# Two output pieces of one head group moved to another sum, with a new order of the work and other streamed weights

## The chip, the cores and the metric

The kernel runs on one core of a Trainium2 chip. TensorE (PE in the profile, with its weight loads as PEld) multiplies into PSUM, VectorE (DVE) and ScalarE (ACT) copy, turn and normalise, GpSimd (POOL) copies small pieces and issues some transfers, and SyncE's queue (SP) issues the large transfers. The metric is the device time of one execution in microseconds; lower is better. The kernel before took 1881.22 us as the median of three runs (1872.94 to 1895.54).

## What is computed

The output has two halves side by side. Half A is a sliding-window attention over 2048 rows; the change leaves it alone. Half B walks over 64 segments of 32 rows. Each segment sees 8 rows of memory ahead of its own 32, and the memory of the next segment is the first 8 rows of this one's output, so the segments run strictly one after the other. Cut to what matters:

```python
mem = mem0                                   # 8 x 640
for s in range(64):
    h = concat([mem, x[32 * s:32 * s + 32]])  # 40 x 640
    q, k, v = h @ Wq, h @ Wk, h @ Wv          # 32 heads of 192
    p = softmax(mask(q @ k.T * scale))        # per head, 40 x 40
    o = (p @ v) @ Wo                          # 6144 x 640, summed over heads
    mem = o[:8]
    out.append(o[8:])
```

## The kernel before

All four weights of half B together are larger than the on-chip memory. They are cut in pieces: for each of four head groups five pieces of Wq, Wk and Wv (128 rows by 1536 columns, 384 KB), and 24 pieces of Wo (320 KB; pieces 0 to 5 belong to head group 0, 6 to 11 to group 1, and so on). Most pieces stay on the chip. The table `STREAMED` (L285) names those that don't: 8 pieces of Wk, 10 of Wv and 5 of Wo, 23 in all, are copied from main memory anew in every segment. `fetch` (L472) issues such a copy on SP's queue into a ring of seven buffers, tile `t`. A copy can therefore start when the piece seven places earlier in the stream has been used for the last time.

One segment works on memory and rows of a segment as 32 new rows (`main`) and as a bundle of 8-row ends that were known early (`ahead`); the bundle is projected for four segments at once, so in each segment one k group and one v group is "renewed" and projected twice (`RENEW`, L288). The order of the work is written out by hand as a list of tokens, `FIRST` for segment 0 and `ORDER` (L298) for the other 63. A token is a step of one head group, and PE, DVE, ACT and SP each run their own instructions in the order of the tokens:

- `q.g`, `k.g`, `v.g`: projections, five pieces each (L561), into one of three PSUM accumulators (`acc`).
- `e.q0` and so on: the copies of accumulators into `QT` or `KT` (L600; the bundle's goes to `sb`, L567). There is one `QT` and one `KT`, so group g + 1 can be copied in only when the scores of group g have been computed. `EVACUATE` (L305) gives the engine of each copy, S for ACT and V for DVE; the first letter is the bundle's copy, which is made in renewed groups alone, and the second the main one.
- `T.q0` and so on: the turning of `QT` or `KT` on DVE (L571), and the late columns by POOL (L607).
- `S.g`: scores on PE (L625). `sb.g`, `mx.g`, `sub.g`, `send.g`: the softmax, on DVE (L631, L638, L642, L647, L648, L657) but for the exponential on ACT (L643). `send.g` writes the tile `P`.
- `tp.g`: P turned by PE (L664). `PT.g`: its spreading, for groups 0 and 1 on ACT (L672) and for groups 2 and 3 on DVE (L675), as `SPREAD` says. `ve.g`: the values copied to `Vst` by ACT (L614).
- `mix.g`: P times V on PE (L688) into two PSUM banks. `ot.g`: these two banks copied as the two halves of `OT` (L696); `HEADS` (L306) names the engine of each half. POOL then collects the late rows of `OT` (L697, L698).
- `out.g.h`: pieces of Wo for group g = 0, 1, 2; h = 0 takes four pieces, h = 1 two (L713). They are summed over the groups in PSUM tile `Y`. A piece has four matmuls of 320 columns. `OT` has twelve slots; pieces 4 and 5 of a group read slots 6 to 11 alone, that is the second half, and the first three pieces of a group read slots 0 to 5 alone.
- `last`: the six pieces of group 3, as 48 matmuls of 160 columns into another layout, `Z` (L739), in a bank of its own.
- `part` (ACT, L720) and `join` (DVE, L725) fold `Y` into the layout of `Z`; the fold lies in `QT`, and its turned form in `KT`. `close` (DVE, L530, L747, L748) turns `Z`, adds the fold, writes the memory rows of the next segment into `HX` and the output rows into `XS`, which POOL sends out (L750). `ql` projects the next q bundle, and the next segment's `q.0` needs what `close` wrote. `tx` (DVE, L530, L541) turns the next segment's rows.

Scores, turned P, mixes and `Z` take their PSUM banks from one ring of four (`bank`), in the order in which they are asked for. A bank is free when its previous content has been read: a score bank when `send` has read it, a mix bank when `ot` has.

Of the kernel before, what the change touches and what calls it, by code (L numbers as in the profile page):

```python
# [23 lines left out]
def part_a(ctx, tc, A_x, A_wqkv, A_wo, out, ident, emit_loads):  # L24
# [241 lines left out]
    with tc.manual_schedule(engines={mybir.EngineType.PE, mybir.EngineType.DVE, mybir.EngineType.Activation}):  # L266
# [4 lines left out]
        for b in range(-1, n_blk):  # L271
# [10 lines left out]

STREAMED = {"q": ((), (), (), ()), "k": ((1, 3), (1, 2), (0, 2), (1, 3)), "v": ((0, 1, 4), (2, 4), (0, 2, 4), (0, 2)),  # L285
            "o": (8, 12, 17, 19, 23)}
PARTS = {}
SLOT = 1536  # L288
RENEW = {0: ("k0", "v2"), 1: ("k1", "v3"), 2: ("k2", "v0"), 3: ("k3", "v1")}
# [6 lines left out]
    ql eql last close Tql  # L296
"""
ORDER = """  # L298
    q.0 e.q0 T.q0 k.0 k.1 e.k0 T.k0 q.1 S.0 sb.0 e.k1 e.q1 mx.0 sub.0 v.0 T.q1 ve.0 T.k1 q.2 S.1 send.0
    e.q2 T.q2 sb.1 mx.1 k.2 tp.0 v.1 e.k2 q.3 PT.0 sub.1 mix.0 T.k2 send.1 tp.1 S.2 ve.1 ot.0 sb.2 e.q3  # L300
    PT.1 mx.2 sub.2 k.3 T.q3 send.2 out.0.0 e.k3 v.2 out.0.1 mix.1 T.k3 S.3 ot.1 tp.2 sb.3 mx.3 v.3 PT.2
    ve.2 mix.2 sub.3 out.1.0 send.3 out.1.1 ot.2 tp.3 ve.3 out.2.0 out.2.1 part tx PT.3 mix.3 ot.3 last
    join ql close eql Tql
"""
EVACUATE = {"k0": "SV", "k1": "SS", "k2": "VS", "k3": "SS", "q0": "VV", "q1": "SS", "q2": "SS", "q3": "VV"}  # L305
HEADS = ("VS", "SV", "VS", "SV")  # L306
SPREAD = "SSVV"
LEAD_IN = 114
HEAD = 10
# [9 lines left out]
def part_b(ctx, tc, B_x, B_mem0, B_Wq, B_Wk, B_Wv, B_Wo, out, ident, n_seg, pre, nbuf, mid):  # L319
    nc = tc.nc  # L320
# [8 lines left out]
    def streamed(u):  # L329
        return u[1] in STREAMED["o"] if u[0] == "o" else u[2] in STREAMED[u[0]][u[1]]  # L330

# [15 lines left out]
    def quarter_cols(u):  # L347
        return 320 if u[0] == "o" else 384
# [11 lines left out]
    def quarter(w, u, i):  # L360

        n = quarter_cols(u)
        if isinstance(w, tuple):
            now = PARTS[u]
            v = w[0][:, n * i:n * i + n] if i < now else w[1][:, n * (i - now):n * (i - now) + n]
            return v.rearrange("p (b c) -> p b c", b=2) if u[0] == "o" else v
        if u[0] == "o":
            return w[:, 640 * (i // 2):640 * (i // 2) + 640].rearrange("p (b g c) -> p g b c", b=2, g=2)[:, i % 2]
        return w[:, n * i:n * i + n]
# [102 lines left out]
    def fetch(u):  # L472
        t = wstream.tile([128, SLOT], BF16, tag="ws")
        nc.sync.dma_start(t[:, 0:stream_cols(u)], copied[u])
        return t[:, 0:stream_cols(u)]
# [3 lines left out]
    def load_pending(u):  # L479
        pending.remove(u)  # L480
        wait.remove(u)
        load_resident([u])

    def get_unit(u):
        if u in wait:
            load_pending(u)
        if not streamed(u):
            return res[u]
        if u in fetched:
            w = fetched.pop(u)  # L490
        else:
            w = fetch(u)
            if pending:
                load_pending(pending[0])
        return (w, res[u]) if u in PARTS else w
# [15 lines left out]
    OT = cpool.tile([128, 12, L], BF16, name="OT")  # L511
# [31 lines left out]
    def bank():  # L543
        return ps_x.tile([128, 512], FP32, tag="x", name="px")
# [50 lines left out]
    def project_qk(s, m, g):  # L595
        return project32([ahead, main] if renewed(s, m, g) else [main], m, g)
# [13 lines left out]
    def values(s, g):  # L610
        return project32([ahead, main] if renewed(s, "v", g) else [main], "v", g)
# [88 lines left out]
    def slot(c):  # L700

        a, k = c // 3, c % 3
        return 6 * (a // 2) + 2 * k + a % 2

    def project_out(Y, g, pairs=range(6)):
        for a in pairs:
            i = 6 * g + a
            w = get_unit(("o", i, 0))
            for r in range(2):
                c = 2 * a + r  # L710
                for gv in range(2):
                    t = 32 * (2 * r + gv)
                    nc.tensor.matmul(Y[t:t + 32].rearrange("p (b c) -> p b c", b=2),  # L713
                                     lhsT=OT[:, slot(c), 0:32], rhs=quarter(w, ("o", i, 0), 2 * r + gv),
                                     start=(i == 0), stop=(i == 17), tile_position=(0, t))

    def join_begin(Y):
        part = QT[:, 0:320].bitcast(FP32)
# [11 lines left out]
        turn32(partT, part)  # L730
        return partT

    def project_last(Y):
        for a in range(6):
            w = get_unit(("o", 18 + a, 0))
            for r in range(2):
                c = 2 * a + r
                for j in range(4):
                    nc.tensor.matmul(Y[32 * j:32 * j + 32], lhsT=OT[:, slot(c), 0:32],  # L739
                                     rhs=quarter(w, ("o", 18 + a, 0), 2 * r + j % 2)[:, j // 2],  # L740
                                     start=(c == 0), stop=(c == 11), tile_position=(0, 32 * j))

    def close(s, Y, part, partT):
        Ysb, T = XS[:], Vst[:, 0:320].bitcast(FP32).rearrange("p (k n) -> p k n", n=SEG)
# [8 lines left out]
    def segment(s):  # L753
        last = s + 1 == n_seg
        engine = {"S": S_, "V": V_}
        got = {}

        def project(m, g):
            if m == "v":
                got["v", g] = values(s, g)  # L760
            else:
                got[m, g] = project_qk(s, m, g)
                if last and (m, g) == ("k", 3):
                    load_late((2, 3))

        def step(name, *at):
            g = int(at[0][-1]) if at else None
            if name in "qkv":
                project(name, g)
            elif name == "e":  # L770
                m = at[0][0]
                got["sb", m, g] = evacuate(m, got.pop((m, g)), [engine[c] for c in EVACUATE[at[0]]])
            elif name == "T":
                m = at[0][0]
                keep = fill_late(s, m, g, got.pop(("sb", m, g)))
                turn_in_place(columns_of(m, 0, 32))
                if m + at[0][1] == "k0" and s and keep:
                    got["keep"] = keep
                elif keep:
                    keep()  # L780
                if at[0] == "k1" and "keep" in got:
                    got.pop("keep")()
            elif name == "S":
                got["S", g] = scores(g)
            elif name == "sb":
                got["t", g] = soft_begin(got.pop(("S", g)))
            elif name == "mx":
                got["mx", g] = soft_max(got["t", g])
            elif name == "sub":
                soft_exp(got["t", g], got.pop(("mx", g)))  # L790
            elif name == "send":
                soft_end(s, g, got.pop(("t", g)))
            elif name == "tp":
                got["p", g] = turn_p(g)
            elif name == "PT":
                got["PT", g] = spread_p(g, got.pop(("p", g)))
            elif name == "ve":
                keep_values(g, got.pop(("v", g)))
                if g == 2:
                    load_x(s + 1)  # L800
                elif last and g == 1:
                    load_late((0, 1))
            elif name == "mix":
                got["mix", g] = mix(g, got.pop(("PT", g)))
            elif name == "ot":
                keep_mix(s, g, got.pop(("mix", g)), [engine[c] for c in HEADS[g]])
            elif name == "out":
                g, half = int(at[0]), int(at[1])
                if "Y" not in got:
                    got["Y"] = ps_y.tile([128, 320], FP32, tag="y", name="Y")  # L810
                project_out(got["Y"], g, range(4 * half, 4 + 2 * half))
            elif name == "part":
                got["part"] = join_begin(got["Y"])
            elif name == "join":
                join_end(got["Y"], got["part"])
                got["partT"] = None if last else turn_part(got["part"])
            elif name == "tx":
                turn_x(s + 1)
            elif name == "ql":
                got["ql"] = None if last else project32([ahead], "q", (s + 1) % 4)  # L820
            elif name == "eql":
                got["sbl"] = None if last else to_sb(got["ql"][0], S_)
            elif name == "last":
                got["Z"] = bank()[:, 0:160]
                project_last(got["Z"])
            elif name == "close":
                close(s, got["Z"], got["part"], got["partT"])
            elif name == "Tql":
                if not last:
                    gl = (s + 1) % 4  # L830
                    turn_late(got["sbl"], "q", gl, s, s + 1)()

        for token in (ORDER if s else FIRST).split():
            step(*token.split("."))
# [3 lines left out]
    def load_late(quads):  # L838
        for b in quads:
            nc.sync.dma_start(res[DEAD[b]], late_o[b].rearrange("p g i c -> p (g i c)"))  # L840
# [143 lines left out]
```

## Time and profile before

| what | value |
|---|---|
| three runs | 1872.94, 1881.22, 1895.54 us |
| the profiled execution, its own time | 1883.37 us |
| its span, first to last instruction | 1881.6 us |
| half A, until half B has its buffers | about 163 us |
| segments 1 to 63, from `last` to `last` | 1608.4 us, 25.53 us each |
| after the last segment (late rows) | 66.4 us |
| PE busy over the span | 1646.5 us, 88% |
| DVE, ACT, POOL busy | 1289.3, 682.5, 680.5 us |
| moved by the transfers | 627.64 MB, 334 GB/s over the span |

How to read it: the busy share of PE counts matmuls that overlap one another and run out in the pipeline, so that 88% doesn't mean that PE can do no more. The segments are one chain, so what matters in them is where PE waits and for whom, and beside it how far the stream of copies is from what the transfer engines can do.

### The profile page before, as it was taken

How to read it: one execution, taken by the hardware profiler on the slowest of the kernel's cores; microseconds unless marked ns; L12 is line 12 of the kernel's file. 1: busy time of each engine (PE TensorE's matmuls, PEld its weight loads, DVE VectorE, ACT ScalarE, POOL GpSimd, SP SyncE). 2: the span in 40 equal slices, each digit the busy share in tenths (PEclk: the TensorE clock that was granted, in tenths of full speed). 3: DMA queues.
4: the chain of work that ended last, by engine and by line, in shares of the span. 5: the costliest groups of instructions: out<-in, count | busy, mean ns of one | idle time of the engine just before them, and what ended most of it. 6: DMA issues, size and time to landing. Idle time of an engine off the chain costs nothing.

```text
span 1881.6 us, 91589 instructions
## 1 busy us (share of the span) xinstructions
PE 1646.5 (88%) x39286; PEld 1043.9 (55%) x39286; DVE 1289.3 (69%) x3671; ACT 682.5 (36%) x1821; POOL 680.5 (36%) x1876
## 2 busy tenths in 40 slices
PE   8998898888888888888888888888889888888887
PEld 5565555555555555555555555555555555555567
DVE  4886677777777777676777777776777777677730
ACT  3454333333333333333333333333333333333310
POOL 3001333344434343433434443433443333444321
PEclk9999999999999999999999999998999999999999
DMA  9926999999999999999999999998999999999991
GB/s 327 317 73 231 388 357 348 360 356 355 348 354 355 355 353 352 340 363 315 361 352 349 363 356 357 372 337 309 369 372 351 360 352 356 333 365 351 348 355 30
DMA packets 276851, 627.64 MB, mean 334 GB/s; under 512 B 60084, under 2 KB 75890, under 8 KB 276444
## 3 DMA queue, kind: packets, MB, share of 16 engines
q1 hardware_dynamic: 257596, 608.42, 90.4%
q0 software_dynamic: 18784, 13.32, 2.3%
q8 instruction: 308, 5.05, 1.1%
q14 instruction: 99, 0.81, 0.1%
q10 hardware_dynamic: 64, 0.04, 0.0%
HBM read 607.47 MB, written 22.91 MB: 335 GB/s over the span
## 4 chain that ended last, share of the span: by engine, by line
PE 54%; DVE 14%; DMA 14%; issue 7%; POOL 6%; ACT 4%; SPq 0%; ACTq 0%; POOLq 0%; DVEq 0%
PE acc L561 27%; DMA t<-wcopy_v 7%; PE Y L713 6%; PE px L625 5%; PE px L688 4%; PE pq L95 3%; DMA late_o<-OL 3%; PE px L739 3%; POOL out_dram L750 2%; DMA t<-wcopy_k 2%; PE px L664 2%; PE px L856 1%; DVE mx L638 1%; DVE px L631 1%; DVE prod L151 1%
## 5 line engine op out<-in xcount | busy, mean ns | idle before, releaser
L561 PEld LDWEIGHTS <-HX 128*32 128x32 bf16 x19380 | 502.3, 97 | 360.2 <-issue 127.0
L561 PE MATMUL acc<-t,HX 128*32 128x384 bf16 x5812 | 435.7, 331 | 32.1 <-DMA t<-wcopy_v 12.6
L561 PE MATMUL acc<-wres_q,HX 128*32 128x384 bf16 x6460 | 326.4, 332 | 22.8 <-issue 11.4
L561 PE MATMUL acc<-wres_k,HX 128*32 128x384 bf16 x3876 | 274.6, 330 | 15.7 <-issue 13.8
L697 POOL COPY OL<-OT 128x96 bf16<-128x96 bf16 x256 | 158.9, 621 | 257.2 <-ACT OT L696 147.8
L561 PE MATMUL acc<-wres_v,HX 128*32 128x384 bf16 x3232 | 215.8, 330 | 2.6 <-issue 2.2
L607 POOL COPY QT<-Lb 128x96 bf16<-128x96 bf16 x252 | 66.7, 265 | 407.0 <-PE px L625 407.0
L696 DVE CAST OT<-px 128x240 bf16<-128x240 f32 x256 | 103.3, 404 | 143.8 <-PE px L688 136.1
L713 PE MATMUL Y<-wres_o,OT 128*32 128x320 bf16 x3840 | 192.7, 302 | 8.6 <-issue 8.3
L625 PE MATMUL px<-KT,QT 64*64 64x40 bf16 (+1 forms) x4096 | 139.3, 189 | 49.6 <-DVE KT L571 23.9
L571 DVE STREAM_TRANSPOSE QT<-QT 128x384 bf16<-128x384 bf16 x256 | 146.6, 573 | 42.2 <-ACT QT L600 40.1
L600 ACT CAST KT<-acc 128x384 bf16<-128x384 f32 x192 | 92.3, 481 | 225.2 <-PE px L625 173.9
L625 PEld LDWEIGHTS <-QT 64*64 64x64 bf16 (+1 forms) x4096 | 108.3, 109 | 111.2 <-issue 46.9
L631 DVE SCALAR_TENSOR_TENSOR px<-px,mask 128x160 f32<-128x160 f32 x256 | 82.7, 323 | 124.0 <-PE px L625 123.7
L698 POOL DMA_DIRECT2D late_o<-OL x256 | 139.4, 545 | 77.9 <-POOL OL L697 60.2
L614 ACT CAST Vst<-acc 128x384 bf16<-128x384 f32 x256 | 123.6, 483 | 110.6 <-PE px L688 87.3
L696 ACT CAST OT<-px 128x240 bf16<-128x240 f32 x256 | 92.4, 361 | 190.0 <-PE px L688 110.7
L567 ACT CAST sb<-acc 128x384 bf16<-128x384 f32 x115 | 55.0, 478 | 262.2 <-PE acc L561 180.5
L713 PEld LDWEIGHTS <-OT 128*32 128x32 bf16 x4608 | 115.1, 97 | 60.7 <-issue 14.4
L571 DVE STREAM_TRANSPOSE KT<-KT 128x384 bf16<-128x384 bf16 x256 | 142.2, 556 | 2.8 <-ACT KT L600 1.2
L750 POOL DMA_DIRECT2D out_dram<-XS x256 | 129.2, 511 | 9.7 <-issue 4.0
L688 PE MATMUL px<-PT,Vst 64*128 64x80 bf16 (+1 forms) x2048 | 123.2, 212 | 9.2 <-issue 6.1
(103 smaller groups left out, 2507.2 us busy)
## 6 DMA issues: line engine op xcount, KB each, us to landing
t<-wcopy_v SPq DMA_DIRECT2D x640, 384.0 KB, 5.9
t<-wcopy_k SPq DMA_DIRECT2D x512, 384.0 KB, 5.5
t<-wcopy_o SPq DMA_DIRECT2D x330, 320.0 KB, 5.3
wres_q<-in_B_Wq_dram SPq DMA_DIRECT2D x20, 384.0 KB, 7.8
late_o<-OL POOLq DMA_DIRECT2D x256, 24.0 KB, 5.1
wres_q<-late_o SPq DMA_DIRECT2D x16, 384.0 KB, 7.3
wres_o<-in_B_Wo_dram SPq DMA_DIRECT2D x19, 320.0 KB, 7.1
wres_k<-in_B_Wk_dram SPq DMA_DIRECT2D x12, 384.0 KB, 7.9
```

The source lines that it names most:

```text
L561: nc.tensor.matmul(ps[n][32 * j:32 * j + 32].rearrange("p (f n) -> p f n", n=32), lhsT=X[:, dc, :], rhs=columns(w, (m, g, dc), j), start=( ...
L571: nc.vector.transpose(t, t)
L600: copies[1](columns_of(m, 0, 32), ps[-1][:].rearrange("p (f n) -> p f n", n=32))
L614: S_(Vst[:], ps[-1][:])
L625: nc.tensor.matmul(Sps[64 * h:64 * h + 64, a, :], lhsT=QT[k0:k1, L * f:L * f + 64], rhs=KT[k0:k1, f, :], start=(outer == 0 and a == 0), st ...
L631: nc.vector.scalar_tensor_tensor(out=Sps, in0=Sps, scalar=scale, in1=mask[:].unsqueeze(1).to_broadcast([128, 4, L]), op0=ALU.mult, op1=ALU ...
L688: nc.tensor.matmul(ps[r][lo:hi, 2 * L * k:2 * L * k + 2 * L], lhsT=V[64 * r:64 * r + 64, col:col + hi - lo], rhs=PT[64 * r:64 * r + 64, 2 ...
L696: copy(OT[:, 6 * r:6 * r + 6].rearrange("p c n -> p (c n)"), ps[r][:, 0:6 * L])
L697: nc.gpsimd.tensor_copy(OL[:, g % 2].rearrange("p n c -> p c n"), OT[:, :, 32:L])
L698: nc.gpsimd.dma_start(late_o[s // 4][:, g, s % 4], OL[:, g % 2].rearrange("p n c -> p (n c)"))
L713: nc.tensor.matmul(Y[t:t + 32].rearrange("p (b c) -> p b c", b=2), lhsT=OT[:, slot(c), 0:32], rhs=quarter(w, ("o", i, 0), 2 * r + gv), sta ...
L750: nc.gpsimd.dma_start(out2[SEG * s:SEG * s + SEG - M, Dm + 160 * j:Dm + 160 * j + 160], Ysb[32 * j + M:32 * j + SEG])
```

## The change

Pieces 16 and 17 of Wo (the last two of group 2, token `out.2.1`) are no longer summed into `Y`. They are written in the layout of `last`, 16 matmuls of 160 columns in place of 8 of 320, into `Z`'s bank, which is now asked for at that token; `last` adds its six pieces to it. `Y` is complete with piece 15. The token moves from ahead of `mix.3` to behind it, and `ot.3` comes after it.

Beside that the whole `ORDER` is written anew. `v.0` comes ahead of `k.1`; `q.1`, `q.2` and `k.2` stand between `S.0` and `S.1`; `q.3` and `k.3` stand ahead of `S.2`; `mix.0` follows `S.2`; `tp.2` follows `v.2`, ahead of `mix.1`; `PT.3` comes ahead of `tx`. The main copies of q0 and q3 go from DVE to ACT, and so do one half of `ot.1` and of `ot.3`; of the bundle's copies, k1's and k3's go to DVE and k2's to ACT. The streamed pieces are others, and they are 10 of Wk, 8 of Wv and 5 of Wo: again 23, of the same bytes.

```diff
-STREAMED = {"q": ((), (), (), ()), "k": ((1, 3), (1, 2), (0, 2), (1, 3)), "v": ((0, 1, 4), (2, 4), (0, 2, 4), (0, 2)),
-            "o": (8, 12, 17, 19, 23)}
+STREAMED = {"q": ((), (), (), ()), "k": ((1, 2), (3, 4), (0, 2, 3), (0, 1, 2)), "v": ((0,), (1, 2), (0, 1, 3), (1, 2)),
+            "o": (8, 15, 17, 21, 23)}
...
 ORDER = """
-    q.0 e.q0 T.q0 k.0 k.1 e.k0 T.k0 q.1 S.0 sb.0 e.k1 e.q1 mx.0 sub.0 v.0 T.q1 ve.0 T.k1 q.2 S.1 send.0
-    e.q2 T.q2 sb.1 mx.1 k.2 tp.0 v.1 e.k2 q.3 PT.0 sub.1 mix.0 T.k2 send.1 tp.1 S.2 ve.1 ot.0 sb.2 e.q3
-    PT.1 mx.2 sub.2 k.3 T.q3 send.2 out.0.0 e.k3 v.2 out.0.1 mix.1 T.k3 S.3 ot.1 tp.2 sb.3 mx.3 v.3 PT.2
-    ve.2 mix.2 sub.3 out.1.0 send.3 out.1.1 ot.2 tp.3 ve.3 out.2.0 out.2.1 part tx PT.3 mix.3 ot.3 last
-    join ql close eql Tql
+    q.0 e.q0 k.0 v.0 e.k0 ve.0 T.q0 k.1 T.k0 S.0 q.1 sb.0 e.k1 mx.0 e.q1 q.2 sub.0 T.q1 k.2 T.k1 S.1
+    send.0 sb.1 tp.0 e.q2 mx.1 e.k2 T.q2 sub.1 T.k2 q.3 k.3 send.1 PT.0 S.2 e.k3 mix.0 tp.1 sb.2 mx.2
+    e.q3 ot.0 sub.2 T.q3 PT.1 v.1 ve.1 out.0.0 send.2 v.2 tp.2 T.k3 mix.1 S.3 out.0.1 PT.2 ot.1 ve.2 v.3
+    sb.3 mx.3 sub.3 mix.2 out.1.0 out.1.1 send.3 ot.2 tp.3 ve.3 PT.3 out.2.0 mix.3 out.2.1 part tx ot.3
+    join last close ql eql Tql
 """
-EVACUATE = {"k0": "SV", "k1": "SS", "k2": "VS", "k3": "SS", "q0": "VV", "q1": "SS", "q2": "SS", "q3": "VV"}
-HEADS = ("VS", "SV", "VS", "SV")
+EVACUATE = {"k0": "SV", "k1": "VS", "k2": "SS", "k3": "VS", "q0": "SS", "q1": "SS", "q2": "SS", "q3": "SS"}
+HEADS = ("SV", "SS", "SV", "SS")
...
-                                     start=(i == 0), stop=(i == 17), tile_position=(0, t))
+                                     start=(i == 0), stop=(i == 15), tile_position=(0, t))
...
-    def project_last(Y):
-        for a in range(6):
-            w = get_unit(("o", 18 + a, 0))
+    def project_sum(Z, which):
+        for i in which:
+            w = get_unit(("o", i, 0))
             for r in range(2):
-                c = 2 * a + r
+                c = 2 * (i % 6) + r
                 for j in range(4):
-                    nc.tensor.matmul(Y[32 * j:32 * j + 32], lhsT=OT[:, slot(c), 0:32],
-                                     rhs=quarter(w, ("o", 18 + a, 0), 2 * r + j % 2)[:, j // 2],
-                                     start=(c == 0), stop=(c == 11), tile_position=(0, 32 * j))
+                    nc.tensor.matmul(Z[32 * j:32 * j + 32], lhsT=OT[:, slot(c), 0:32],
+                                     rhs=quarter(w, ("o", i, 0), 2 * r + j % 2)[:, j // 2],
+                                     start=(i == 16 and r == 0), stop=(i == 23 and r == 1), tile_position=(0, 32 * j))
...
-                project_out(got["Y"], g, range(4 * half, 4 + 2 * half))
+                if (g, half) == (2, 1):
+                    got["Z"] = bank()[:, 0:160]
+                    project_sum(got["Z"], (16, 17))
+                else:
+                    project_out(got["Y"], g, range(4 * half, 4 + 2 * half))
...
             elif name == "last":
-                got["Z"] = bank()[:, 0:160]
-                project_last(got["Z"])
+                project_sum(got["Z"], range(18, 24))
```

## The prediction

> **What bounds the kernel now.** I read the page's head first, then the busy time by stretches, then PE's waits.
>
> ```profile
> span 1881.6 us, 91589 instructions
> PE 1646.5 (88%) x39286; PEld 1043.9 (55%) x39286; DVE 1289.3 (69%) x3671; ACT 682.5 (36%) x1821; POOL 680.5 (36%) x1876
> ```
>
> The change touches the segments. The view by stretches takes segments 1 to 63 as one stretch, then single ones; the last three columns are PE's granted clock, the share of the 16 transfer engines and GB/s.
>
> ```profile
> 206.80:1815.20 1608.40, 1409.93 (x35064) 875.65 (x35060) 1144.40 (x3481) 585.72 (x1622) 634.35 (x1763) 0.99 0.98 353
> 845.00:870.60 25.60, 20.44 (x491) 12.64 (x485) 15.97 (x51) 8.54 (x24) 9.74 (x28) 0.93 0.90 302
> 1355.70:1381.20 25.50, 23.50 (x624) 15.14 (x624) 19.97 (x63) 8.95 (x26) 10.68 (x29) 1.00 1.02 379
> 1381.20:1406.70 25.50, 23.12 (x588) 14.77 (x588) 18.68 (x57) 9.88 (x27) 10.77 (x30) 1.00 1.02 376
> ```
>
> 63 segments in 1608.4 us are 25.53 us each. The transfer engines are busy 98% of it, so the stream of copies stands close behind PE; but 353 GB/s is not the most they do: two neighbouring stretches moved 379 and 376. The stream gives way a little when its buffers come free earlier. At 353 GB/s a segment moves 9.01 MB, before and after.
>
> PE's waits in the same stretch (us in total, times, longest):
>
> ```profile
> PE px L739 <- ACT OT L696: 37.1, 62, 0.6
> PE acc L561 <- issue: 33.4, 49, 2.3
> PE px L625 <- DVE KT L571: 23.9, 40, 0.9
> PE px L625 <- POOL QT L607: 13.4, 15, 3.1
> PE acc L561 <- DMA t<-wcopy_v: 11.5, 27, 1.3
> PE acc L561 <- ACT sb L567: 9.3, 9, 2.6
> PE acc L561 <- ACT KT L600: 5.2, 17, 0.4
> PE acc L561 <- DMA t<-wcopy_k: 5.0, 14, 0.7
> PE px L664 <- DVE P L657: 2.4, 11, 0.5
> ```
>
> Waits on other engines: 37.1 + 23.9 + 13.4 + 9.3 + 5.2 + 2.4 = 91.3 us, or 1.45 us a segment. Waits for copies: 16.5 us, 0.26 a segment. So PE's chain sets the pace, and the stream stands close behind. "issue" is PE's own stall, which the change can't touch.
>
> **The change, part by part.** I lay both orders out by hand, for a segment in which nothing is renewed, with these durations: a chain of the trace from one group's scores to the next, and three lengths of PE.
>
> ```profile
> 1004.18 0.56 PE px L625 x16
> 1004.76 0.34 DVE px L631
> 1005.13 0.34 DVE mx L638
> 1005.49 0.33 DVE px L642
> 1005.82 0.48 DVE QT L571
> 1006.30 0.47 DVE KT L571
> 1006.77 0.14 issue
> 1006.91 0.54 PE px L625 x16
> 1008.37 0.22 PE px L664 x2
> 1010.47 0.45 PE px L688 x16
> 1024.54 4.98 PE acc L561 x120
> ```
>
> A projection of 20 matmuls is 4.98 / 6 = 0.83 us of PE. Scores end at 1004.74 and the next start at 1006.91. The groups of instructions by line give the rest (mean ns after the comma):
>
> ```profile
> L696 DVE CAST OT<-px 128x240 bf16<-128x240 f32 x252 | 101.7, 404 | 143.1 <-PE px L688 135.4 <-PE Y L713 7.3
> L657 DVE TENSOR_TENSOR P<-px,sm 128x128 bf16<-128x128 f32 x504 | 98.2, 236 | 14.0 <-PE acc L561 0.5 <-PE px L688 0.5
> L647 DVE TENSOR_REDUCE sm<-px 128x4 f32<-128x160 f32 x252 | 77.5, 307 | 28.2 <-ACT px L643 28.2
> L648 DVE RECIPROCAL sm<-sm 128x4 f32<-128x4 f32 x252 | 44.9, 178 | 8.7
> L600 DVE CAST QT<-acc 128x384 bf16<-128x384 f32 x126 | 67.7, 537 | 6.0 <-PE acc L561 5.8
> L675 DVE TENSOR_TENSOR PT<-px,own 128x320 bf16<-128x320 f32 x126 | 60.5, 480 | 0.1
> L600 ACT CAST QT<-acc 128x384 bf16<-128x384 f32 x126 | 60.7, 482 | 58.1 <-PE px L625 54.8 <-DVE P L657 3.3
> L696 ACT CAST OT<-px 128x240 bf16<-128x240 f32 x252 | 90.9, 361 | 190.0 <-PE px L688 110.7 <-PE Y L713 77.9
> ```
>
> `send` is 0.31 + 0.18 + two overlapping P = 0.9 us of DVE.
>
> *S.1.* Before, v.0 and q.2 (1.66) stand between the scores, against 2.17 us of DVE: a wait of 0.5 to 0.65. After, q.1, q.2 and k.2 stand there (2.49), but q.1 is only copied when it is done: 0.83 + 0.48 on ACT, then T.q1, T.k1 and 0.14, 2.6 together: a wait of 0.15.
>
> *tp.0.* Before it has k.2 as cover. After, it stands right behind S.1, and send.0 follows T.k1: a new wait of 0.4. Behind it on PE stand q.3 and k.3.
>
> *S.2.* Before covered. After, DVE has sb.1, mx.1, T.q2, sub.1 and T.k2 (2.1) behind send.0, PE has tp.0, q.3 and k.3 (1.9): 0.3.
>
> *mix.0.* The second of its banks is, in the ring of four, now that of S.1, free when send.1 has read it; before it was that of S.0. send.1 ends 0.4 after S.2: a wait of 0.4. tp.1, next, needs send.1 anyway, and waited 0.55 for it before, behind a mix.0 that was not held.
>
> *S.3, mix.2, tp.3.* Before, DVE carried e.q3 and the half of ot.1 ahead of T.k3 and send.3: 0.7, 0.25 and 0.25. After, those 0.54 and 0.40 are ACT's, and k.3 is projected two steps earlier: 0, 0.1 and 0. In all DVE loses two copies of 0.537 and two of 0.404, 1.88 us, and ACT gains 2 x 0.482 + 2 x 0.361 = 1.69 us a segment. ACT was busy 585.72 of 1608.40 us, so its idle time covers it; without that cover the whole 1.69 would stand in the chain.
>
> *The end.* The timeline ahead of `last`:
>
> ```profile
> 1021.58 0.59 ACT L720 COPY QT<-Y 64x160 f32<-64x160 f32 x2 [0.67 <-PE Y L713]
> 1022.60 0.32 PE L739 MATMUL px<-wres_o,OT 128*32 128x160 bf16 x8 [0.63 <-ACT OT L696]
> 1022.75 0.31 PE L739 MATMUL px<-t,OT 128*32 128x160 bf16 x8
> ```
>
> A piece in Z's layout takes 0.15 us, so the moved pieces take 0.30. As many columns ran before, in half as many matmuls: I charge nothing, and bound it by -0.05 and +0.1. They read slots 6 to 11 alone, so the first half of ot.3 can be copied beside them, and the first three pieces of `last` need only that half; the second half, ACT's too, follows the moved pieces by 0.4 and is wanted 0.45 after `last` begins. `part` (0.59) now ends about when the mix does. The wait was 0.5 to 0.63 and becomes 0.15. But mix.3 has lost this cover: PT.3 (0.48, ahead of `tx` now, behind ot.2's half of 0.40) is late by 0.25. Laid out by hand, before it was late by 0.55, behind `tx`.
>
> *Sum by hand.* Before: S.1 0.65, tp.1 0.55, S.3 0.7, mix.2 0.25, tp.3 0.25, mix.3 0.55, last 0.5 = 3.45. After: S.0 0.15 (T.q0 now behind e.k0), S.1 0.15, tp.0 0.4, S.2 0.3, mix.0 0.4, mix.2 0.1, mix.3 0.25, last 0.15 = 1.9. The trace has 1.45 where I lay out 3.45, since in PE's own stalls the other engines catch up: 42% comes through. Then 1.9 gives 0.80, and the order is worth 0.65 us a segment, 41 us. Ends: 0 (all of the new waits come through in full, 1.9 against 1.45 even costs 0.45) and 1.1, if the 1.45 shrank to the 0.35 of POOL's rows and the bundle's.
>
> *The streamed pieces.* 23 copies of the same bytes: nothing by count. For 0.65 us less the stream must move 9.01 MB in 24.88 us, 362 GB/s; the trace has 353 in the mean and 377 at its best over 51 us. 362 is 9 of 24 up that way, so I let three fifths of the gain stand, 25 us, and give 16 back to waits for copies. Ends: nothing stands, or all.
>
> *POOL and SP.* POOL's order is not written by hand; its late columns of QT cost 13.4 us in 15 waits and I leave them, with 10 us to both sides. On SP the load of XS moves ahead of v.3's pieces: if XS were still being sent, all later copies would queue behind it. It is asked for behind v2's last piece, which waits for k3's first to be used, in the middle of the segment, when the last segment's rows are long out; so I charge nothing. In renewed segments the bundle's k1 and k3 go over DVE (0.54 in one segment of two, some within waits): 0.1 a segment, in the ends.
>
> 1883.4 (the profiled execution's own time; the median of the runs shown is 1881.2, 2 less) minus 25 is 1858; on the median 1856. I take 1857.
>
> The Trainium skill, "DMA: Bandwidth & Descriptors", section Specifications, gives main memory about 358 GB/s per core. By that the sum would be 9.01 MB / 358 = 25.17 us a segment, 23 us in all, 1859, and nothing below could be reached. The trace's 379 and 376 don't agree with it as a ceiling, so the sum and the low end go by the rows.
>
> **Rivals.**
>
> *The copies eat it.* The wait moves from DVE to `t`: 1872 to 1888, say 1880. For it: the share of 98%. Against it: PE waited for copies only 16.5 us.
>
> *Slower: one starved piece.* The streamed pieces now come in threes. A copy starts when the piece seven places back is done. For v2's last streamed piece that is k3's first; between them PE has the rest of k.3 (0.7), S.2, mix.0, tp.1, v.1, out.0.0 (0.6) and most of v.2, 3.9 us, in two of four segments, in the others 4.5 and 5.3. Before, the shortest such distance is 4.9, for k2's pieces. Stretched as a segment is (25.53 for 20.4 of PE's work, 1.25), 3.9 is 4.8 us.
>
> ```profile
> t<-wcopy_v SPq DMA_DIRECT2D x640, 384.0 KB, 5.9
> DMA to landing us min/median/max: 2.8/5.5/8.5
> ```
>
> At 5.9 the piece is late by 1.1 us. Over a segment, with smaller lacks at v1 and k1, 1.2 to 1.5 us less the 0.65: +0.5 to +0.85, 32 to 54 us, say 1915. It decides from a landing at which the lateness exceeds 0.65 over all segments, about 5.5 us for that piece. Against it: ahead of k3's first PE runs 1.8 us without a release, so the queue has run down and landing should be nearer the 2.8 than the 8.5; and new waits at S.2 and mix.0 lie just there and give it time.
>
> **How the numbers follow.** The forecast, 1835 to 1872, gets 0.52; below it 0.04; the eaten gain, 1872 to 1888, 0.20; the starved piece, or new waits in full, above 1888, 0.24. A measurement of this kernel can tell about 1% from no change: under 1862 or over 1900. Of the forecast 0.36 lies under 1862, with what is below it 0.40; above 1900 I put 0.22; between them 0.38. The range, 1835 to 1905, leaves out 0.04 below and 0.16 above.
>
> **What would show it.** Right: the wait of L739 for ACT under 15 us; DVE's KT ahead of L625 no longer among the great waits; PE idle ahead of L664 and L688 for DVE's P; DVE near 1025 us in segments 1 to 63, ACT near 690; GB/s near 359. Waits for `t` grown from 16.5 to some 30 us mean the first rival in part, past 60 with v2's pieces the second. Wrong: a long wait behind POOL, or the same waits of L739.

## The result and the profile after

| kernel | median | runs | ratio to before, 95% interval |
|---|---|---|---|
| before | 1888.11 us | 1872.94 to 1895.54 (6) | |
| after | 1910.49 us | 1902.25 to 1924.26 (6) | 1.0133 [1.0094, 1.0171] |

The changed kernel is 1.3% slower, about 25 us, and the interval leaves "no change" out, where 1857 us and a range up to 1905 were forecast. The profiled execution after took 1915.77 us. Its page gives, with the queue that brings the instructions, the chain of waits by engine and by line, and the landing of v's streamed pieces:

```profile
span 1913.9 us, 92605 instructions
PE 1658.1 (87%) x39798; PEld 1054.5 (55%) x39798; DVE 1185.6 (62%) x3430; ACT 772.4 (40%) x2062; POOL 687.7 (36%) x1876
q8 instruction: 312, 5.11, 1.1%
PE 48%; DMA 27%; DVE 8%; POOL 7%; issue 6%; ACT 4%; SPq 0%; POOLq 0%; ACTq 0%; DVEq 0%
t<-wcopy_v SPq DMA_DIRECT2D x512, 384.0 KB, 6.0
```

The same chain line and queue line of before:

```profile
q8 instruction: 308, 5.05, 1.1%
PE 54%; DVE 14%; DMA 14%; issue 7%; POOL 6%; ACT 4%; SPq 0%; ACTq 0%; POOLq 0%; DVEq 0%
```

In the chain that sets the end DVE falls from 14% to 8%, as was meant, and DMA rises from 14% to 27%. Segments 1 to 63 as one stretch:

```profile
209.30:1844.50 1635.20, 1416.07 (x35550) 882.59 (x35548) 1043.33 (x3246) 673.84 (x1860) 641.57 (x1763) 0.99 0.97 347
```

A segment takes 1635.20 / 63 = 25.96 us, 0.43 more. DVE has lost 101 us of work there and ACT has gained 88, where the layout by hand gives 118 (1.88 x 63) and 106 (1.69 x 63), and the stream is no faster: 347 GB/s, before 353. PE's waits over the whole run:

```profile
PE acc L561 <- DMA t<-wcopy_v: 61.8, 116, 1.9
PE acc L561 <- issue: 45.3, 55, 2.7
PE px L625 <- POOL QT L607: 16.1, 19, 2.3
PE acc L561 <- ACT sb L567: 13.1, 14, 4.0
PE px L739 <- issue: 8.8, 11, 1.8
PE acc L561 <- DMA t<-wcopy_k: 8.4, 14, 1.6
PE px L688 <- issue: 8.4, 8, 1.7
PE px L625 <- DVE KT L571: 8.0, 15, 0.6
```

L739's wait for ACT, 37.1 us before, is not among the great ones; in the segments it is 2.1 us:

```profile
PE px L739 <- ACT OT L696: 2.1, 8, 0.4
```

All rows of this view, added up by what PE waited for ("other" is other engines and the other transfers):

| whole run, us | issue | copies into `t` | other |
|---|---|---|---|
| before | 69.8 | 19.7 | 118.3 |
| after | 72.9 | 73.2 | 73.2 |

45 us of waits for engines are gone, and 53.5 us of waits for copies have come. PE's timeline of one segment, from k.3 to v.2, shows where some of them stand:

```profile
1048.40 0.66 PE L561 MATMUL acc<-t,HX 128*32 128x384 bf16 x12
1048.89 0.50 PE L561 MATMUL acc<-wres_k,HX 128*32 128x384 bf16 x8
...
1051.27 0.72 PE L713 MATMUL Y<-wres_o,OT 128*32 128x320 bf16 x16
1051.81 0.34 PE L561 MATMUL acc<-t,HX 128*32 128x384 bf16 x4
1052.52 0.35 PE L561 MATMUL acc<-t,HX 128*32 128x384 bf16 x4 [0.37 <-DMA t<-wcopy_v]
1052.69 0.35 PE L561 MATMUL acc<-wres_v,HX 128*32 128x384 bf16 x4
1053.79 0.35 PE L561 MATMUL acc<-t,HX 128*32 128x384 bf16 x4 [0.76 <-DMA t<-wcopy_v]
```

k3's three streamed pieces (the `x12`) are used from 1048.40 on. v2's last piece stands seven places behind k3's first in the stream, so its copy may start when the first four of the twelve matmuls are done, about 1048.7, and it is wanted at 1053.0, after 4.3 us. Such copies land 6.0 us after their issue (the median above), and PE stands still for v2's second piece (0.37) and third (0.76). This is the rival "one starved piece", at its place. Counted stand by stand in the trace, some 34 of the 62 us of waits for `wcopy_v` lie at v.2, and some 23 at v.3, which the rival didn't name. But starved pieces are not the whole of the loss, as the experiments show.

### The profile page after: what moved, and what is told of

It is laid out like the page before. It is cut to its first block, busy times and chain, and to the rows that moved or that the text cites. A ratio compares the mean times of both kernels' runs of the same rounds, so it can differ in the third digit from the quotient of the medians.

```text
span 1913.9 us, 92605 instructions
## 1 busy us (share of the span) xinstructions
PE 1658.1 (87%) x39798; PEld 1054.5 (55%) x39798; DVE 1185.6 (62%) x3430; ACT 772.4 (40%) x2062; POOL 687.7 (36%) x1876
## 4 chain that ended last, share of the span: by engine, by line
PE 48%; DMA 27%; DVE 8%; POOL 7%; issue 6%; ACT 4%; SPq 0%; POOLq 0%; ACTq 0%; DVEq 0%
PE acc L561 24%; DMA t<-wcopy_v 17%; DMA late_o<-OL 6%; PE Y L713 4%; PE px L625 4%; PE pq L95 3%; PE px L688 3%; POOL out_dram L750 3%; PE px L739 2%; DMA t<-wcopy_k 2%; PE px L664 2%; PE px L859 1%; POOL OL L697 1%; DVE QT L571 1%; POOL Lb L591 1%
## 5 line engine op out<-in xcount | busy, mean ns | idle before, releaser
L561 PEld LDWEIGHTS <-HX 128*32 128x32 bf16 x19380 | 514.3, 97 | 442.5 <-issue 208.0
L561 PE MATMUL acc<-t,HX 128*32 128x384 bf16 x5812 | 381.9, 329 | 80.8 <-DMA t<-wcopy_v 61.8
L561 PE MATMUL acc<-wres_q,HX 128*32 128x384 bf16 x6460 | 317.3, 334 | 31.3 <-issue 22.5
L561 PE MATMUL acc<-wres_v,HX 128*32 128x384 bf16 x3880 | 248.3, 328 | 9.2 <-issue 9.0
L696 ACT CAST OT<-px 128x240 bf16<-128x240 f32 x384 | 137.2, 362 | 273.0 <-PE px L688 146.1
L561 PE MATMUL acc<-wres_k,HX 128*32 128x384 bf16 x3228 | 213.7, 328 | 19.2 <-ACT sb L567 12.4
L600 ACT CAST QT<-acc 128x384 bf16<-128x384 f32 x256 | 122.8, 480 | 198.8 <-PE px L625 119.4
L713 PE MATMUL Y<-wres_o,OT 128*32 128x320 bf16 x3584 | 181.3, 303 | 3.5 <-issue 3.0
L625 PE MATMUL px<-KT,QT 64*64 64x40 bf16 (+1 forms) x4096 | 138.3, 189 | 37.8 <-POOL QT L607 16.1
L625 PEld LDWEIGHTS <-QT 64*64 64x64 bf16 (+1 forms) x4096 | 108.4, 109 | 111.5 <-issue 45.7
L675 DVE TENSOR_TENSOR PT<-px,own 128x320 bf16<-128x320 f32 x128 | 62.2, 486 | 120.6 <-PE px L688 112.8
L688 PE MATMUL px<-PT,Vst 64*128 64x80 bf16 (+1 forms) x2048 | 122.7, 213 | 7.8 <-issue 2.9
L713 PEld LDWEIGHTS <-OT 128*32 128x32 bf16 x4096 | 93.5, 96 | 50.1 <-DVE OT L696 10.2
```

Of the source, the lines that this page charges most:

```text
L561: nc.tensor.matmul(ps[n][32 * j:32 * j + 32].rearrange("p (f n) -> p f n", n=32), lhsT=X[:, dc, :], rhs=columns(w, (m, g, dc), j), start=( ...
L600: copies[1](columns_of(m, 0, 32), ps[-1][:].rearrange("p (f n) -> p f n", n=32))
L625: nc.tensor.matmul(Sps[64 * h:64 * h + 64, a, :], lhsT=QT[k0:k1, L * f:L * f + 64], rhs=KT[k0:k1, f, :], start=(outer == 0 and a == 0), st ...
L688: nc.tensor.matmul(ps[r][lo:hi, 2 * L * k:2 * L * k + 2 * L], lhsT=V[64 * r:64 * r + 64, col:col + hi - lo], rhs=PT[64 * r:64 * r + 64, 2 ...
L696: copy(OT[:, 6 * r:6 * r + 6].rearrange("p c n -> p (c n)"), ps[r][:, 0:6 * L])
```

## The experiments

Four questions in turn: which part of the change costs, what "issue" is, what the new order is worth by itself, and what takes its gain. Ratios are to the kernel before on the same chip.

**The streamed pieces.** First the changed order with pieces spread evenly (e1_even):

```diff
-STREAMED = {... "k": ((1, 2), (3, 4), (0, 2, 3), (0, 1, 2)), "v": ((0,), (1, 2), (0, 1, 3), (1, 2)), "o": (8, 15, 17, 21, 23)
+STREAMED = {... "k": ((1, 4), (2, 4), (0, 1, 4), (0, 2, 3)), "v": ((1,), (0, 4), (3, 4), (1, 2, 4)), "o": (11, 13, 17, 19, 23)
```

> The changed kernel's order with other streamed pieces (k: 1,4 / 2,4 / 0,1,4 / 0,2,3; v: 1 / 0,4 / 3,4 / 1,2,4; o: 11,13,17,19,23), again 23 of the same bytes, chosen so that no piece has much less than 5.8 us between the use of the piece seven places ahead and its own (v2's last had 5.25 us in the mean in the changed kernel). Starved piece: PE's waits for copies fall from 71 us to 30-45, the time to 1860-1885, below the kernel before. Rate (the stream as a whole can't go faster, wherever the pieces lie): the waits only move to other pieces, 55-70 us in all, 1895-1910. Order (the new waits in the order itself): 1895-1910 with waits for copies well down and others up.

Measured: 1906.31 us, 1.0094 [1.0071, 1.0118]. PE's waits over the whole run:

```profile
PE acc L561 <- issue: 65.1, 66, 2.7
PE acc L561 <- DMA t<-wcopy_v: 18.9, 35, 2.0
PE px L739 <- issue: 15.4, 15, 2.2
PE px L625 <- issue: 10.1, 12, 1.3
PE Y L713 <- issue: 10.1, 12, 1.5
```

The waits for copies fall from 73.2 to 25.0 us in all, as the starved piece wanted; but the time falls by some 7 us only (1.0133 to 1.0094, with intervals that overlap), for "issue" rises from 72.9 to 112.2. So something else stood right behind. It isn't the engines: waits for these and for other transfers stay at 72.3 us. The other two exchanges, the changed kernel with the pieces of before (e2_old_streams) and the kernel before with the changed pieces (e3_new_streams), each an exchange of the line `STREAMED`:

> The changed kernel's order with the streamed pieces of the kernel before. In this order k1's first and second piece and v0's last stand only 3.7 to 4.4 us behind the piece seven places ahead. Starved piece: slower than the changed kernel by 0.6 to 1.5 us a segment, 1950-2005, with the waits at k1 and v0 and none left at v2. Rate or order: as the changed kernel, 1900-1920.

> The kernel before with the streamed pieces of the changed one. In the old order k3's third, v2's last and v3's second stand 4.2 to 4.6 us behind the piece seven places ahead. Starved piece: slower than the kernel before by 0.8 to 1.6 us a segment, 1940-1990, waits for copies at k3, v2, v3. Rate: as before, 1880-1890. Order: as before, since the order is the old one.

Measured: e2 1923.06 us, 1.0184 [1.0159, 1.0209]; e3 1933.53 us, 1.0239 [1.0211, 1.0268]. The largest waits for copies, of e2 and then of e3:

```profile
PE acc L561 <- DMA t<-wcopy_k: 51.8, 91, 2.0
PE acc L561 <- DMA t<-wcopy_v: 21.3, 46, 1.1
```

```profile
PE acc L561 <- DMA t<-wcopy_v: 79.9, 123, 2.4
```

Pieces that don't fit the order cost 0.9% in the new order (e2 against e1) and 2.4% in the old one (e3 against before). The starved theory was right in kind, and in the new order it foresaw too much (1950 to 2005 us).

**The end of a segment alone.** The kernel before, with pieces 16 and 17 in `Z` and the end of `ORDER` as after (e4_tail_only):

```diff
-    ... out.2.0 out.2.1 part tx PT.3 mix.3 ot.3 last join ql close eql Tql
+    ... PT.3 out.2.0 mix.3 out.2.1 part tx ot.3 join last close ql eql Tql
-HEADS = ("VS", "SV", "VS", "SV")
+HEADS = ("VS", "SV", "VS", "SS")
```

> The kernel before with the end of the segment alone as in the change: pieces 16 and 17 in Z's bank between mix.3 and ot.3, PT.3 ahead of out.2.0, part and tx behind, ot.3 with both halves on ACT; order ahead of it, evacuations and streamed pieces as before. The step by the prediction: the wait ahead of last falls from 0.79 us (first matmul of last behind the matmul before it) to about 0.3, mix.3 waits 0.15 more, so 0.2 to 0.35 us a segment, 13 to 22 us, of which the stream may take back up to half: 1865-1882. Rival: PT.3's wait and part on ACT cost as much as the end gains: 1883-1895.

Measured: 1890.22 us, 1.0018 [0.9999, 1.0037]. From 206 to 1840 us, nearly all of the segments:

```profile
PE acc L561 <- issue: 43.4, 54, 2.0
...
PE px L739 <- issue: 16.3, 17, 1.9
PE px L625 <- POOL QT L607: 12.8, 16, 2.9
PE px L739 <- ACT OT L696: 10.9, 51, 0.4
```

L739's wait for ACT fell from 37.1 to 10.9 us, and no time was gained: "issue" rose there from 2.6 to 16.3 us. So I asked what "issue" is.

**What "issue" is.** PE's timeline of before, a stall inside one resident piece of Wk, with the same rows and the same accumulator, and nothing to wait for:

```profile
1011.94 0.33 PE L561 MATMUL acc<-wres_k,HX 128*32 128x384 bf16 x1
1013.42 0.34 PE L561 MATMUL acc<-wres_k,HX 128*32 128x384 bf16 x3 [1.16 <-issue]
```

The theory, to be tested: PE's instructions come in blocks over the same transfer engines as the copies, and a late block stops PE. The change adds 8 matmuls with their weight loads, 16 instructions a segment. So two kernels add instructions to the one before without changing data, order or pieces: pieces 16 and 17 cut into matmuls of 160 columns but still summed into `Y` in the old place (e5_split_two, 16 more), and pieces 1 to 17 (e6_split_all, 136 more):

```diff
+                    if i >= 16:          # e6: if i > 0
+                        for b in range(2):
+                            nc.tensor.matmul(Y[t:t + 32, 160 * b:160 * b + 160],
+                                             lhsT=OT[:, slot(c), 0:32], rhs=quarter(w, ("o", i, 0), 2 * r + gv)[:, b],
+                                             start=False, stop=(i == 17 and b == 1), tile_position=(0, t))
+                        continue
```

> The kernel before, with pieces 16 and 17 still summed into Y at the old place, but each of their matmuls of 320 columns cut into two of 160: 16 PE instructions (8 matmuls, 8 weight loads) more in each segment, the same columns, nothing else. Instructions (PE can't get its instructions faster than one block of 256 in about 5 us while the copies run, so more instructions cost time even where they have no more columns): 10 to 25 us slower, the waits called issue up. Prediction's charge of nothing: within 5 us of the kernel before.

> The same cut for pieces 1 to 17: 136 PE instructions more in each segment (12%), the same columns. Instructions: half a block more of 256 a segment at about 5 us each, 1.5 to 2.8 us a segment, 95 to 175 us slower. Charge of nothing: within 15 us of the kernel before.

Measured: e5 1899.65 us, 1.0073 [1.0042, 1.0104], about 14 us; e6 1997.43 us, 1.0594 [1.0537, 1.065], about 112 us. For e6 the instruction queue, and PE's largest issue waits from 206 to 1700 us:

```profile
q8 instruction: 342, 5.60, 1.1%
```

```profile
PE Y L715 <- issue: 40.2, 37, 2.4
...
PE acc L561 <- issue: 25.0, 31, 2.1
PE px L745 <- issue: 24.2, 17, 2.5
```

34 more packets (342 - 308) for 136 x 64 = 8704 more instructions: 256 a packet. After has 16 x 64 / 256 = 4 more, 312. Issue waits are 142.1 us in e6, against 69.8. e4 adds the same 16 instructions as e5; if they cost e5's 0.73% there too, its end gained about 0.55%.

The traces, which keep each packet of this queue, bear the theory out stall by stall. Number PE's records, matmuls and weight loads, in order of time: of the 140 stands of PE over 0.6 us in before, 53 end at the same place in a block of 256 records, and no other place has more than two. The stall shown above ends there. Stands at that place (over 0.3 us) come to 65.9 us in before, 75.5 in after, 115.6 in e1 and 139.2 in e6, where "issue" is 69.8, 72.9, 112.2 and 142.1. In before nine of ten of them end 1.26 to 1.65 us after the end of a packet of that queue. So in these four kernels "issue" is, nearly all of it, PE waiting for the next block.

Not all of e6's 112 us are such waits. PE's own busy time grew from 1646.5 to 1707.2 us with the same columns, and the granted clock fell from 0.987 to 0.956 in the profiled executions. By the traces' clock records PE ran at half clock for 41 us of before's segments, in 11 spells, and for 150 us of e6's, in 37; each spell began within 4 us of a stand of PE of 0.8 us or more. So a long stand seems to cost twice here: by itself, and, behind some of them, by a spell of mostly 3.4 us at half clock.

**The order with light copies.** Of each group's streamed pieces of Wk and Wv only the first is copied, and the others read its buffer; so 10 of 23 copies, and the content of those pieces, are left out. On the kernel before (e7_few_before) and on e1_even (e8_few_new):

```diff
+    def shared(u):
+        return u[0] in "kv" and u[2] != STREAMED[u[0]][u[1]][0]
...
+        if shared(u):
+            return got_of[u[0], u[1]]
```

> The kernel before, which copies only the first streamed piece of each k and v group in a segment and lets the others read that buffer, so it leaves out 10 of 23 copies (and the content of those pieces): the transfer engines are far from full and no piece can starve. Instructions: with the engines free PE's instruction blocks come sooner too, the waits called issue fall under 20 us; 1780 to 1830. Chain alone (only the 17 us of waits for copies go): 1865-1880.

> The changed order with the even streamed pieces, with the same 10 of 23 copies left out. If the order's chain is shorter as the prediction laid it out (0.65 us a segment, 41 us) and only copies and instruction blocks hid that, it comes out 25 to 60 us below the kernel before with the copies left out. If the order itself costs what it gains, the two are within 15 us.

Measured: e7 1777.25 us, 0.9419 [0.938, 0.9458]; e8 1735.56 us, 0.9196 [0.9155, 0.9236]. The new order is 41.7 us faster here. PE's waits of e7 over the whole run, then of e8 (lines are 7 further down):

```profile
PE px L746 <- ACT OT L703: 38.5, 63, 0.6
PE px L632 <- DVE KT L578: 25.0, 43, 0.9
...
PE px L632 <- issue: 13.4, 33, 0.9
...
PE acc L568 <- issue: 3.7, 7, 1.1
```

```profile
PE acc L568 <- issue: 25.4, 34, 2.2
PE px L632 <- DVE KT L578: 8.0, 14, 0.6
```

There is no wait for a copy into `t` in either. Waits for engines and other transfers are 119.8 us in e7 and 64.5 in e8; issue is 20.6 and 32.9. Two more kernels take e7 as their base: with e6's cut (e10_few_split), and with the changed end (e11_few_tail):

> The kernel before with 10 of 23 copies left out (1777) and the matmuls of pieces 1 to 17 cut in two, 136 PE instructions more in each segment. With the copies running this cut cost 111 us. Instruction blocks held up by the full transfer engines: with the engines a third free it costs less than half of that, under 50 us, 1780-1827. PE's own cost of a matmul: about the same 111 us, 1880-1895.

> The kernel before with 10 of 23 copies left out (1777) and the changed end of the segment alone. With the copies running this end came out at 1.0018 of the kernel before. The prediction's step (0.2 to 0.35 us a segment, 13 to 22 us, covered up by the 16 instructions there): 1755-1767. If the end gains nothing by itself: 1772-1785.

Measured: e10 1797.64 us, 0.9527 [0.9492, 0.9563]; e11 1764.69 us, 0.9359 [0.9317, 0.94]. The 136 instructions that cost 112 us cost 20 here: issue rises by 8.5 us (20.6 to 29.1), PE's busy time by 14.0 (1608.4 to 1622.4), and the clock stays at 0.99. So PE's own work on them is the small part of the 112; the larger is how their blocks arrive beside full transfer engines, with the clock that is lost behind the stalls. The end alone gains 12.6 us (0.7% of e7's time, near the 0.55% put down to e4's), all of the new order 41.7.

**What takes the gain.** First e1_even with pieces 16 and 17 back in `Y`, 16 instructions fewer, the rest of the new order kept (e9_new_in_Y):

```diff
-    ... PT.3 out.2.0 mix.3 out.2.1 part tx ot.3
+    ... PT.3 out.2.0 out.2.1 mix.3 part tx ot.3
```

> The changed order with the even streamed pieces, but pieces 16 and 17 summed into Y again with 8 matmuls of 320, ahead of mix.3, so 16 PE instructions fewer in each segment than with the even pieces alone, and the wait ahead of last uncovered again. Instructions (a ceiling of its own while the copies run): 8 to 18 us below the changed order with even pieces (1906), 1888-1898, although the chain at the end is longer. Chain: 10 to 20 us above it, 1916-1926.

Measured: 1901.29 us, 1.0081 [1.005, 1.0112]. Against e1's 1.0094 the intervals overlap, so it tells little: fewer instructions, but L739 waits for ACT again:

```profile
PE px L739 <- ACT OT L696: 38.9, 63, 0.6
```

Then fewer instructions without losing the end: the pieces in `Z` as matmuls of 320 columns, over e1_even (e12_wide_Z, eight pieces, 64 fewer), the kernel before (e13_wide_Z_before, six pieces, 48 fewer) and the changed kernel with its own pieces (e14_wide_Z_after, 64 fewer). The columns are the same; what is left out is the right layout of these sums.

```diff
-                for j in range(4):
-                    nc.tensor.matmul(Z[32 * j:32 * j + 32], lhsT=OT[:, slot(c), 0:32],
-                                     rhs=quarter(w, ("o", i, 0), 2 * r + j % 2)[:, j // 2],
+                for j in (2 * r, 2 * r + 1):
+                    nc.tensor.matmul(Z[32 * j:32 * j + 32].rearrange("p (b c) -> p b c", b=2),
+                                     lhsT=OT[:, slot(c), 0:32], rhs=quarter(w, ("o", i, 0), j),
```

> The changed order with the even streamed pieces (1906), all copies running, but the eight pieces summed into Z as 4 matmuls of 320 columns each in place of 8 of 160: the same columns of PE, 64 PE instructions (5.6%) fewer in each segment. It leaves out the right layout: the sums lie in the wrong places. Instructions as the ceiling that took the gain of the new order: at 13 us for 16 instructions up to 52 us less, 1855-1880, below the kernel before. The copies' rate as the ceiling: 1893-1906, with the waits for copies grown from 21 to 40 us or more.

> The kernel before with last's six pieces as 4 matmuls of 320 columns each in place of 8 of 160: 48 PE instructions fewer in each segment, the same columns; it leaves out the right layout of these sums. If instruction blocks hold up both orders alike: 48/64 of the 33 us that the new order gained from 64 fewer, 25 us, 1855-1867. If the old order is held by its own waits and the blocks come while PE waits: 1877-1890, and then the blocks took the new order's gain in particular.

> The changed kernel with its own streamed pieces and the eight pieces of Z as 4 matmuls of 320 columns each: 64 PE instructions fewer in each segment; it leaves out the right layout. Against the even pieces with the same cut (1873) this is the cost of the starved pieces by themselves, not covered by instruction blocks. Starved piece, as first read from the waits (50 us more of them): 1905-1925. Starved pieces that mostly take time in which the blocks would have held PE up anyway: 1875-1895.

Measured: e12 1873.21 us, 0.9906 [0.9872, 0.994]; e13 1864.32 us, 0.9919 [0.9887, 0.9951]; e14 1885.57 us, 1.0004 [0.9981, 1.0027]. Fewer instructions make all three faster, by 0.8 to 1.9%. e12 and e13 have the same number of instructions (before less 48) and pieces that fit their order, and they run equally fast, though e12's chain is some 41 us shorter by e7 and e8. 1394 us of the segments of each, by stretch (last columns: clock, share of the transfer engines, GB/s), e12 and then e13:

```profile
206.00:1600.00 1394.00, 1239.23 (x29406) 755.28 (x29402) 915.67 (x2843) 591.23 (x1630) 563.16 (x1542) 0.98 0.98 356
```

```profile
206.00:1600.00 1394.00, 1232.44 (x29466) 757.68 (x29462) 1004.00 (x3055) 514.18 (x1422) 561.44 (x1554) 0.99 0.99 358
```

| whole run, us | issue | copies into `t` | other |
|---|---|---|---|
| e12_wide_Z (new order) | 48.3 | 53.2 | 86.0 |
| e13_wide_Z_before (old order) | 33.8 | 31.2 | 127.2 |

41.2 us fewer waits for engines; 22.0 more for copies and 14.5 more for instructions. Beside that PE is busy 13.8 us longer in e12 (1655.1 against 1641.3) with the same columns, at a granted clock of 0.977 against 0.986: 65 us of its segments at half clock, against 41. That is where the order's gain goes. e14 against e12 differs in the pieces alone: 1.0004 against 0.9906, so once instructions hold up less, the changed kernel's pieces cost 1.0%, some 18 us. PE's largest wait for a copy, e14 and then e12:

```profile
PE acc L561 <- DMA t<-wcopy_v: 60.3, 107, 2.5
```

```profile
PE acc L561 <- DMA t<-wcopy_v: 27.6, 48, 2.2
```

## Why the prediction was wrong

*The step that failed: "I let three fifths of the gain stand, 25 us, and give 16 back to waits for copies".* Nothing stands. The trust in 362 GB/s came from single stretches at 379 and 376; over the segments e13, with all 23 copies and a share of 0.99, held 358, and the changed kernel 347. Waits for copies rose from 19.7 to 73.2 us, by 53.5 and not by 16, past the 60 that was named as the mark of the second rival. That rival had the place (v2's pieces), and its time, 1915 against 1910, is luck: its price, 32 to 54 us net of the gain, is not what the pieces cost by themselves, which is 7 us against e1's pieces, and 18 where instructions hold up less. The reason given against it, that the queue would have run down and a copy land nearer 2.8 us, finds no support: v's pieces land after 6.0 us in the median. And where e1 takes the waits for copies away, waits for instructions stand behind them, which the prediction didn't have.

*The order, 0.65 us a segment, 41 us: right in size, in part by luck.* With light copies it is worth 41.7 us, and in the changed kernel PE's waits on other engines fell by 45. But the 42% sets 1.45 us of waits against a layout that doesn't have 0.36 of them (POOL's 13.4 us and the bundle's 9.3, over 63 segments); without these 32% comes through, and the order would be worth 0.49 us a segment, 31 in all. And new waits of 0.4 us a segment each were laid out at tp.0 and mix.0, with PE idle ahead of L664 and L688 for DVE's P as the sign: weight loads of L664 waited 16.1 us for P in the whole run, before 29.7, and those of L688 not at all. DVE at 1043 us (near 1025 forecast), ACT at 674 (near 690) and DVE's KT ahead of L625 at 8.0 us fit.

*The end of a segment: right in kind.* Its two terms, `last` and mix.3, are worth (0.35 + 0.30) x 0.42 = 0.27 us, 17 in all, by the layout, and 12.6 us with light copies; L739's wait for ACT was forecast under 15 us and is 2.1.

*"As many columns ran before, in half as many matmuls: I charge nothing, and bound it by -0.05 and +0.1": wrong, a term mis-sized.* 16 more instructions cost 14 us with everything else in its place, 0.22 us a segment, above the upper bound. That bound was taken from matmul durations, and as far as these go it holds: in the profiled executions PE is busy 5.5 us longer in e5 (0.09 a segment), and 9.2 more are "issue".

*"'issue' is PE's own stall, which the change can't touch": wrong, and the reason for the former.* The stalls are PE waiting for instructions, and a change touches them by each instruction that it adds (e5, e6), and by how full the transfer engines are (69.8 us before, 20.6 in e7).

*The sum.* Of the 25 us lost, e5 gives 14 to the 16 instructions (in the old order) and e1 gives 7 to the pieces, if the two add up; the other 4 lie within the intervals. The order's 41 us is given back in waits for copies and instructions, and in clock. How it divides is shown for e12 against e13 alone (22 and 14.5 us of waits, 13.8 of PE's busy time); for the changed kernel it stays open, for waits for copies and for instructions trade places, as e1 shows. Why only some long stands lower the clock stays open too. A version with wide matmuls in `Z` and the right layout wasn't made; its fold at the end would cost something again.

## What to carry to other kernels

When a stream of copies keeps the transfer engines 97 to 99% busy, as in these runs, a shorter chain of waits may not come out as time, as none of it did here: first make the stream lighter or its instructions fewer, and test an order's worth with some copies left out. Count the instructions that a change adds on the engine that sets the pace, not only its columns, and suspect a wait for instructions where "issue" stands inside a run of equal matmuls; what shows it is that the stands come back at the same place of every 256 instructions. For a ring of buffers, take the time between the use that frees a buffer and the use of what is copied into it, and compare it with the measured landing for each piece whenever the order of uses moves.

## What the runs showed of the hardware that was not expected

PE's instructions come 256 to a packet of 16.4 KB (5.05 MB / 308), and beside 353 GB/s of copies 16 more of them in a segment of some 1110 ((35064 + 35060) / 63, matmuls and weight loads before) cost 0.73% of the time, 136 more cost 5.9%; on top of e7, which moves 213 GB/s at a share of 0.67, the same 136 cost 20 us instead of 112:

```profile
206.00:1700.00 1494.00, 1361.68 (x34866) 858.80 (x34858) 1133.19 (x3463) 583.79 (x1616) 636.21 (x1755) 1.00 0.67 213
```

The packet of the next block starts, in the median, 2.8 us after PE has entered the block ahead of it in before, and 1.3 us in e7; it takes 1.0 us in both, and PE enters a block that it had to wait for some 1.4 us (median) after the packet's end. By these medians the next block is there some 5.2 us (2.8 + 1.0 + 1.4, an estimate) after PE has entered the last in before, and some 3.7 in e7; where PE is done with 256 instructions sooner, it stands.

The Trainium skill, "Runtime: NRT & Kernel Launch", section Instruction fetch mechanics, says that instructions are refilled in blocks of 16 KiB, 256 instructions, and that crossing a block is mostly hidden. The size agrees with this case's 256 and 16.4 KB; that it is hidden holds neither with full transfer engines (69.8 us of issue waits before, 142.1 in e6) nor wholly with light ones (20.6 in e7).
